# Sliding-window scores in four 64x64 array tiles, with a narrower key band and two shifted copies of V

## The chip, the cores and the metric

The kernel runs on one core of a Trainium2 chip. The metric is the device time of one execution in microseconds (us), lower is better. A run's state is fast or slow, judged by its time against the fastest of the same kernel; only fast runs are compared here.

## The reference

Attention with a window of 128 keys and an ALiBi bias (8 batches, 8 heads, 576 positions, 64 wide), followed by a feed-forward step on the 4608 tokens:

```python
rel    = pos[:, None] - pos[None, :]
bias   = slopes[:, None, None] * (-np.abs(rel))[None]
mask   = (rel >= 0) & (rel < 128)
scores = np.where(mask, q @ k.T / sqrt(64) + bias, -1e9)     # per batch and head
attn   = softmax(scores)
x      = (attn @ v), heads side by side                      # 4608 x 512
h      = x @ w_in                                            # 512 -> 2048
out    = (h * np.cos(h)) @ w_out                             # 2048 -> 512
```

## The kernel before

All operations are listed first; then a small scheduler inside the kernel (`Plan`) plays them through in its own clock and fixes, for good, the order of the instructions on each engine. For that it uses **booked durations** that stand with each operation: `occ` is the time until the engine can take the next one, `lat` the time until the result is there. At run time there is no other order: each engine runs its list from the front, and stops where an operand is not ready.

```python
def op(self, eng, fn, r=(), w=(), dma=None, occ=100, lat=None, pri=5, ...):   # list one operation
...
    o.start = st                     # in schedule(): the booked times, and with them the order
    free[e] = st + o.occ
    ...
        o.end = st + o.lat
```

A batch of attention has eight units of a head pair and 256 queries, four with G = 0 (the first 256 positions) and four with G = 1, and a tail of 64 queries. They go in groups of three through scores (TensorE), exp (ScalarE), mask (VectorE), PV (the product of the exponentials, P, with V; TensorE) and norm (VectorE). Between these steps TensorE runs **filler**: the large matmuls of the feed-forward step, in chunks of 512 tokens.

```python
def scores(us):                                          # two row tiles, x = 0, 1: the two heads of a pair
    ...
    jobs = [(128, 384, 2 * G, 2 * G, 2), (384, 512, 2 * G + 1, 2 * G + 1, 1)]
    if G:
        jobs.append((0, 128, 2 * G - 1, 2 * G, 1))
    for (c0, c1, kc, qb, nb) in jobs:
        for x in range(2):
            ins = e.matmul(ps[:, banks[x], c0:c1], keys_ap(i, x, pr, kc),
                           query_ap(i, x, pr, qb, nb), start=True, stop=True)
    ...
    occ += 250 if u[0] == "t" else 220 if u[1] else 165

def mask(b, u):                                          # G = 1: one instruction; G = 0: two
    ...
    op("dve", lambda e: e.tensor_tensor(p, p, m, ALU.mult), ..., occ=605, lat=lat, pri=1)

def pv(b, u, s):                                         # per query block: diagonal and previous key block
    ...
    ins = e.matmul(o, P[i][:, x, d0:d0 + 128], V[:, kc, h, 0:65], start=True, stop=not two)
    if two:
        ins = e.matmul(o, P[i][:, x, p0:p0 + 128], V[:, kc - 1, h, 0:65], start=False, stop=True)
```

V is loaded one to two batches ahead, by DMAs that GpSimd issues, behind certain transposes:

```python
if c == 1:
    load_v(2, after=crossed[3:4])
    load_qk(3)
    load_v(3)
...
if 3 < c + 2 < B:
    load_v(c + 2, after=xops[3:4] if c > 2 else xops[-1:])
```

The softmax here doesn't subtract the row's maximum and nothing guards it: scores larger than these inputs give would overflow.

## Time and profile before

Median of three runs 313.91 us (313.4 to 314.86). The profiled execution has a span of 311.4 us at a granted clock of 1.0.

| | before |
|---|---|
| TensorE busy | 302.1 us, 97% of the span |
| VectorE busy | 196.8 us, 63% |
| ScalarE busy | 206.7 us, 66% |
| share of the chain that ended last | TensorE 86%, DMA 8%, VectorE 1% |
| first scores of batches 2 to 7 start at | 73.16, 104.47, 134.78, 165.62, 198.73, 229.43 us |

"The chain that ended last" is followed back from the last instruction, at each step to whatever released it. A chain that is nearly all TensorE means that the other engines are in time nearly everywhere. Batches count from 0. (The prediction calls the batch at 134 us "batch 5"; it is batch 4. Nothing hangs on it. Where it speaks of a score group "before and after the change alike", it means the change of tiling mode at the group's two ends.)

### The profile page before, as it was taken

To read this page: it belongs to the slowest core of one execution; us is meant where nothing else is said; L and a number is where in the kernel's file an instruction comes from. 1 tells how busy PE (TensorE), PEld (TensorE's weight loads), DVE (VectorE), ACT (ScalarE), POOL (GpSimd) and SP (SyncE) were. 2 spreads that over 40 slices of the span, in tenths; PEclk is the share of its full clock that TensorE was granted. 3 is DMA by queue.
4 is the path that set the end of the run, shared out by engine and by line. 5 is a ranking of instruction groups with operands and counts; after the bars stand their busy time and mean duration, and the time that the engine had idled before them with its cause. 6 is when DMAs were issued, how large, how long until landed. Compare 5 with 4: busy or idle time off the path is not lost.

```text
span 311.4 us, 6714 instructions
## 1 busy us (share of the span) xinstructions
PE 302.1 (97%) x2647; PEld 178.0 (57%) x2684; DVE 196.8 (63%) x444; ACT 206.7 (66%) x303; POOL 105.8 (34%) x134
## 2 busy tenths in 40 slices
PE   8799999999999999999999999999999999999996
PEld 4578546785578557845854554455445544444444
DVE  3798675786568757875887458766866882353000
ACT  7798936787588759773986488848873884462211
POOL 8999820069506300870537055505000000000000
DMA  9999999999939992999999999999823200101112
GB/s 131 166 193 193 192 171 193 164 105 167 189 76 121 154 171 47 120 152 191 141 175 158 176 138 108 147 169 138 144 59 103 70 8 2 68 0 67 69 67 101
DMA packets 159742, 38.97 MB, mean 125 GB/s; under 512 B 147808, under 2 KB 155232, under 8 KB 159712
## 3 DMA queue, kind: packets, MB, share of 16 engines
q0 software_dynamic: 109552, 18.10, 80.0%
q1 hardware_dynamic: 50160, 20.46, 33.5%
q8 instruction: 21, 0.34, 0.5%
q14 instruction: 9, 0.07, 0.1%
HBM read 36.70 MB, written 9.44 MB: 148 GB/s over the span
## 4 chain that ended last, share of the span: by engine, by line
PE 86%; DMA 8%; POOL 3%; issue 1%; DVE 1%; ACT 0%; POOLq 0%
PE ps L863 37%; PE ps L837 20%; PE ps L852 18%; DMA qnat<-in_q_dram 6%; PE ps L631 4%; PE ps L725 3%; DMA knat<-in_k_dram 2%; PE ps L728 2%; POOL vp L463 1%; PE ps L800 1%; PE ps L711 1%; PE ps L546 1%; PE ps L713 1%; PE ps L621 1%; POOL qnat L427 0%
## 5 line engine op out<-in xcount | busy, mean ns | idle before, releaser
L863 PE MATMUL ps<-w_outb,gT 128*128 128x512 bf16 (+2 forms) x564 | 133.7, 373 | 2.2 <-issue 0.8
L829 DVE TENSOR_TENSOR gT<-ps,cos 128x512 bf16<-128x512 f32 x144 | 94.8, 686 | 27.7 <-PE ps L863 14.0
L823 ACT ACTIVATE cos<-ps,halfpi 128x512 f32<-128x512 f32 x144 | 94.9, 687 | 20.9 <-PE ps L837 6.7
L863 PEld LDWEIGHTS ps<-w_outb,gT 128*128 128x128 bf16 x592 | 52.6, 98 | 53.1 <-issue 1.4
L668 ACT ACTIVATE p<-ps 128x768 bf16<-128x768 f32 (+1 forms) x64 | 54.8, 919 | 27.5 <-PE ps L631 15.3
L852 PE MATMUL ps<-xT,w_inb 128*128 128x256 bf16 x576 | 67.5, 273 | 0.0
L837 PE MATMUL ps<-xT,w_inb 128*128 128x512 bf16 x280 | 63.9, 379 | 0.6
L463 POOL DMA_DIRECT2D vp<-in_v_dram x40 | 34.8, 909 | 79.8 <-DMA xT<-xnat 35.2
L852 PEld LDWEIGHTS ps<-xT,w_inb 128*128 128x128 bf16 x576 | 54.5, 98 | 7.2 <-issue 0.5
L837 PEld LDWEIGHTS ps<-xT,w_inb 128*128 128x128 bf16 x288 | 27.3, 98 | 32.2 <-DVE xtail L756 1.1
L419 ACT ACTIVATE ob<-ps 128x512 f32<-128x512 f32 (+2 forms) x24 | 14.0, 582 | 44.2 <-PE ps L863 44.2
L454 POOL DMA_DIRECT2D qnat<-in_q_dram x32 | 29.3, 915 | 26.1 <-DMA xT<-xtail 26.1
L686 DVE TENSOR_TENSOR p<-p,emask 128x1024 bf16<-128x1024 bf16 x32 | 22.0, 688 | 13.7 <-ACT p L668 13.5
L454 POOL DMA_DIRECT2D knat<-in_k_dram x32 | 29.3, 917 | 2.1 <-PE ps L713 2.1
L767 DVE TENSOR_TENSOR xnat<-ps,rec 128x256 bf16<-128x256 f32 x64 | 26.8, 421 | 2.0
L725 PEld LDWEIGHTS ps<-vp,p 128*128 128x128 bf16 x256 | 17.0, 97 | 15.0 <-issue 8.8
L725 PE MATMUL ps<-vp,p 128*128 128x65 bf16 x256 | 21.9, 193 | 0.5 <-DVE p L686 0.4
L691 DVE TENSOR_TENSOR p<-p,emask 128x256 bf16<-128x256 bf16 x32 | 9.1, 283 | 17.6 <-ACT p L668 17.1
L728 PE MATMUL ps<-vp,p 128*128 128x65 bf16 x192 | 20.0, 193 | 0.0
L491 ACT ACT_TABLE_LOAD x15 | 19.2, 1283 | 0.3
L631 PEld LDWEIGHTS ps<-qt,kt 64*128 64x128 bf16 x320 | 12.0, 95 | 11.5 <-issue 7.8
L631 PE MATMUL ps<-qt,kt 64*128 64x128 bf16 (+1 forms) x320 | 18.4, 241 | 0.1
(58 smaller groups left out, 173.8 us busy)
## 6 DMA issues: line engine op xcount, KB each, us to landing
out_dram<-ob SPq DMA_DIRECT2D x35, 256.0 KB, 3.8
vp<-in_v_dram POOLq DMA_DIRECT2D x32, 128.0 KB, 5.9
knat<-in_k_dram POOLq DMA_DIRECT2D x25, 128.0 KB, 8.9
qnat<-in_q_dram POOLq DMA_DIRECT2D x25, 128.0 KB, 7.7
w_inb<-in_moe_w_in_dram POOLq DMA_DIRECT2D x8, 256.0 KB, 9.0
w_outb<-in_moe_w_out_dram POOLq DMA_DIRECT2D x6, 256.0 KB, 15.1
qnat<-in_q_dram POOLq DMA_DIRECT2D x3, 256.0 KB, 10.6
knat<-in_k_dram POOLq DMA_DIRECT2D x3, 256.0 KB, 13.3
```

The costliest lines, as they stand in the source:

```text
L454: op("pool", [lambda e: e.dma_start(nat[w][b % 2][0:rows, t, :].rearrange("p (h d) -> p h d", h=H), src[b, :, 128 * t:128 * t + rows, :].r ...
L463: op("pool", [lambda e, t=t, rows=rows: e.dma_start(vp[b % 2][0:rows, t, :, 0:64], v[b, :, 128 * t:128 * t + rows, :].rearrange("h p d -> ...
L631: ins = e.matmul(ps[:, banks[x], c0:c1], keys_ap(i, x, pr, kc), query_ap(i, x, pr, qb, nb), start=True, stop=True)
L668: op("act", lambda e: e.activation(P[i][:, :, lo:512], src_[:, :, lo:512], ACTF.Exp, scale=0.125), w=held + [("P", i)], occ=920 if u[1] el ...
L725: ins = e.matmul(o, P[i][:, x, d0:d0 + 128], V[:, kc, h, 0:65], start=True, stop=not two)
L728: ins = e.matmul(o, P[i][:, x, p0:p0 + 128], V[:, kc - 1, h, 0:65], start=False, stop=True)
L767: op("dve", lambda e: e.tensor_tensor(o, U[:, :, :, 0:64], rv[:, :, :, None].broadcast_to([128, 2, 2, 64]), ALU.mult), r=[("rec", ri)], w= ...
L823: op("act", lambda e: e.activation(cosb[ci][:, :], h, ACTF.Sin, bias=halfpi[:, 0:1]), r=["halfpi"], w=[("B", bank), ("cos", ci)], occ=586, ...
L829: op("dve", lambda e: e.tensor_tensor(o, h, cs, ALU.mult), r=[("cos", ci)], w=[("B", bank)] + keys, occ=606, lat=692, pri=3)
L837: op("pe", lambda e, kc=kc: e.matmul(ps[:, bank, :], w_in[:, kc, 128 * fc:128 * fc + 128], xT[:, kc, CH * c:CH * c + CH], start=(kc == 0), ...
L852: op("pe", lambda e, i=i, fc=fc, kc=kc: e.matmul(ps[:, bank, 256 * i:256 * i + 256], w_in[:, kc, 128 * fc:128 * fc + 128], xT[:, kc, t0:t0 ...
L863: op("pe", lambda e, fc=fc: e.matmul(ps[:, bank, 0:wd], gT[gi][:, fc, 128 * t:128 * t + 128], w_out[:, fc, c0:c0 + wd], start=(fc == 0), s ...
```

## The change

Its intent: a block of 128 queries needs at most 255 keys, but a block of 64 queries needs only 191. Cut the queries in blocks of 64, and a band of 192 keys does. Scores, exp and masks then touch 192 in place of 256 keys per query, and the scores run in four 64x64 tiles of the array in place of two 64x128. The keys of a query block now start at multiples of 64, so PV needs V shifted by 64 positions too: `vx`, made by four VectorE copies per batch. The part of P that belongs to only one half of a block is masked into a zeroed tile `Ph`, by instructions on 64 partitions. Batches 0 and 1 stay as they were. The core of the diff, with cuts marked by "..." and three comments added:

```diff
+QUART = 2
+        Ph = [sb(f"ph{i}", [128, 2, 2, 128]) for i in range(NH)]
+        vx = sb("vx", [128, 6, H, VW])
+        def dense_masks(behind):                           # set-up, once, ahead of batch 2
+            for j in range(2):
+                ... e.tensor_copy(EM[a:a + 64, :, 256:384], EM[a:a + 64, :, c:c + 128]) ... occ=330, lat=400, pri=6
+            for i in range(NH):
+                ... e.memset(Ph[i][:, :, :, :], 0.0) ... occ=200, lat=270, pri=6
+        def shifted_v(b):                                  # V's shifted copies, four per batch
+            for j in range(2):
+                a = 64 * j
+                for n, (o, t) in enumerate(((0, 1 - j), (3, j))):
+                    op("dve", lambda e, a=a, o=o, t=t: e.tensor_copy(
+                        vx[a:a + 64, o:o + 3, :, :], V[a:a + 64, t:t + 3, :, :]),
+                       ... occ=480, lat=560, pri=4)
         def scores(us):
+                    if b >= QUART:
+                        for pr, j, c, kb, ks, qb, q0, n in quarters(b, u):
+                            for x in range(2):
+                                rows = slice(64 * x, 64 * x + 64)
+                                ins = e.matmul(ps[64 * j:64 * j + 64, banks[x], c:c + n],
+                                               tr["k"][i][rows, kb, pr, 64 * ks:64 * ks + 64],
+                                               tr["q"][i][rows, qb, pr, q0:q0 + n], ...)
         def mask(b, u):                                    # the G = 1 case
+                    e.tensor_tensor(p[:, :, :, 0:128], p[:, :, :, 0:128], EM[... 256:384] ..., ALU.mult)
+                    for j in range(2):
+                        a = slice(64 * j, 64 * j + 64)
+                        ins = e.tensor_tensor(
+                            Ph[n][a, :, :, 64 * j:64 * j + 64], p[a, :, :, 128:192],
+                            EM[a, hh, None, 192 * j:192 * j + 64].broadcast_to([64, 2, 2, 64]), ALU.mult)
+                op("dve", f, ..., occ=750 if G else 620, lat=835 if G else 705, pri=1)
         def pv(b, u, s):
+                            e.matmul(o, P[i][:, x, 192 * rb:192 * rb + 128],
+                                     vx[:, Q - 1, h, 0:65], start=True, stop=False)
+                            ins = e.matmul(o, Ph[hbuf[(b, u)]][:, x, rb, :],
+                                           vx[:, Q + 2, h, 0:65], start=False, stop=True)
+                    if c + 1 == QUART:
+                        dense_masks([o for o in R.all if o.eng[0] == "dve"][-1:])
...
+                    shifted_v(c + 1)
```

## The prediction

> **What bounds the kernel now.** I read the page's busy shares first, then the chain that ended last, then the groups by shape, and last the timelines of TensorE and VectorE around one batch (batch 5, from 134 us). From the page, the busy shares and the chain by engine:
>
> ```profile
> PE 302.1 (97%) x2647; PEld 178.0 (57%) x2684; DVE 196.8 (63%) x444; ACT 206.7 (66%) x303; POOL 105.8 (34%) x134
> ...
> PE 86%; DMA 8%; POOL 3%; issue 1%; DVE 1%; ACT 0%; POOLq 0%
> ```
>
> TensorE is the bound: 97% busy, and 86% of the chain. The other engines have a third of the span free. So TensorE time saved counts in full, while work added to VectorE is free only as long as no TensorE instruction has to wait for it. The groups that the change touches, from the groups by shape (count | busy us, mean ns of one | idle before):
>
> ```profile
> L668 ACT ACTIVATE p<-ps 128x1024 bf16<-128x1024 f32 x32 | 31.0, 1026 | 13.3 <-PE ps L621 11.9 <-PE ps L631 1.4
> L668 ACT ACTIVATE p<-ps 128x768 bf16<-128x768 f32 x32 | 24.4, 812 | 14.1 <-PE ps L631 13.9
> L686 DVE TENSOR_TENSOR p<-p,emask 128x1024 bf16<-128x1024 bf16 x32 | 22.0, 688 | 13.7 <-ACT p L668 13.5
> L631 PE MATMUL ps<-qt,kt 64*128 64x256 bf16 x128 | 15.4, 277 | 0.1
> L631 PE MATMUL ps<-qt,kt 64*128 64x128 bf16 x192 | 14.6, 218 | 0.0
> L693 DVE TENSOR_TENSOR p<-p,emask 128x512 bf16<-128x512 bf16 x32 | 13.4, 419 | 0.0
> L691 DVE TENSOR_TENSOR p<-p,emask 128x256 bf16<-128x256 bf16 x32 | 9.1, 283 | 17.6 <-ACT p L668 17.1
> ```
>
> The whole of the scores is only 30.0 us of overlapping matmul time in 311 us, so nothing here can be large. TensorE's timeline for the first score group of batch 5 (start, length, what) gives its real cost:
>
> ```profile
> 134.78 0.67 PE L631 MATMUL ps<-qt,kt 64*128 64x256 bf16 x12
> 135.38 1.90 PE L863 MATMUL ps<-w_outb,gT 128*128 128x512 bf16 x8
> 137.12 0.26 PE L725 MATMUL ps<-vp,p 128*128 128x65 bf16 x3
> ...
> 140.24 0.78 PE L631 MATMUL ps<-qt,kt 64*128 64x256 bf16 x16
> 140.95 0.82 PE L863 MATMUL ps<-w_outb,gT 128*128 128x512 bf16 x3
> ```
>
> Read start to start: the group of three G=0 units holds TensorE from 134.78 to 135.38, 0.60 us, the second group (one G=0, two G=1) 0.71 us. Filler (L863) runs while ScalarE and VectorE work, then the PV matmuls (L725) come. VectorE at the same place:
>
> ```profile
> 136.33 0.29 DVE L691 TENSOR_TENSOR p<-p,emask 128x256 bf16<-128x256 bf16 x1 [1.10 <-ACT p L668]
> 136.54 0.42 DVE L693 TENSOR_TENSOR p<-p,emask 128x512 bf16<-128x512 bf16 x1
> 137.03 0.29 DVE L691 TENSOR_TENSOR p<-p,emask 128x256 bf16<-128x256 bf16 x1
> 137.24 0.42 DVE L693 TENSOR_TENSOR p<-p,emask 128x512 bf16<-128x512 bf16 x1
> 137.57 0.18 DVE L765 RECIPROCAL rec<-ps 128x4 f32<-128x4 f32 x1
> ```
>
> The first mask ends at 136.54 + 0.42 = 136.96 and its PV starts at 137.12: 0.16 us later. Over all 72 units that distance is 0.06 to 0.25 us nearly everywhere. The static order puts each PV just where its mask is ready, and within a group VectorE works without a gap. **There is almost no slack between a mask and its PV**, though VectorE is only 63% busy.
>
> **What the Trainium skill says.** "TensorEngine Tiling (Array Packing)", Key Properties: tiles run independently, and a change of tiling mode drains the array. The trace agrees with the second: about 0.1 us is lost on each side of a score group, before and after the change alike. "TensorE: Matmul & The Clock Gate", Part 3, has row and column tiles compose; this trace shows two row tiles (scores) and two column tiles (the 32 transposes from 47.08 to 48.10 us start 0.03 us apart, half of what 128 columns take), never four tiles. "VectorE: DVE Perf Modes", the perf-mode tier table: 16-bit tensor_tensor gets two elements a cycle, a copy within SBUF four. The masks agree: 256, 512 and 1024 elements take 283, 419 and 688 ns, 0.53 ns per element and 0.15 us fixed. The same page, "Two Vector instructions with no wait between them": an instruction whose operands start in another 32-partition quadrant than those of the one before is held until all earlier ones have finished. Nearly all of this kernel starts at partition 0; the one case with a start at 64 is a memset at the beginning (third column "DVE", then line):
>
> ```profile
> 1.42 0.27 DVE L513 MEMSET vp<- 64x256 uint32 x1
> 1.77 0.09 DVE L515 MEMSET ptail<- 128x32 uint32 x1
> 1.83 0.17 DVE L516 MEMSET kt<- 128x128 uint32 x1
> ```
>
> The one after the partition-64 memset starts 0.08 us behind its end, the next starts 0.03 us before the end of its predecessor. That agrees, but another memset pair with no such change also waited, so the trace does not settle it.
>
> **The change part by part** (batches 2 to 7, so six times; each has four G=0 and four G=1 units and a tail).
>
> Scores, TensorE. Before, each of two row tiles streams 384 columns for a G=0 and 512 for a G=1 unit. After, each of four tiles streams 320 and 384. The tail stays at 512 (32 small matmuls for 16). Per batch 4 x 64 + 4 x 128 = 768 columns less. A column costs 0.42 ns (512-column matmuls start 0.216 us apart). So 0.32 us a batch, **1.9 us in all**, if four tiles really run side by side. The number of matmuls rises by 10 per G=1, 8 per G=0 and 16 per tail: 88 x 6 = 528, each with a weight load. They cost start time (about 3 ns between partners), so I count 1.5 us. PV keeps its count and its 65 columns: 0. Mode switches: as many as before.
>
> Exp, ScalarE: 1024 to 768 elements takes 1026 to 812 ns; 768 to 640, at the same 0.84 ns per element, 812 to 705. Per batch 4 x 0.214 + 4 x 0.107 = 1.28 us, 7.7 us in all, off the path.
>
> Masks, VectorE. G=1: one 688 ns instruction becomes three: 512 elements (419) and two of 256 on 64 partitions (283 each), 985 in sum. G=0: 283 + 419 = 702 becomes 419 + 2 x 221 (128 elements: 0.15 us + 128 x 0.53 ns) = 861. Per batch 4 x 0.30 + 4 x 0.16 = 1.8 us. V's copies: 4 a batch of 1584 elements, at four a cycle 412 ns + 0.15 = 0.56 us, 2.2 us a batch. In all 24 us more, plus 2 us of set-up: VectorE from 197 to about 223 us, 71%. Not the bound as a total.
>
> But each mask lies between exp and PV. In the old kernel instructions overlap: a 256-element mask's successor starts 0.21 us after it (136.33 to 136.54), 0.07 less than its length. The scheduler that fixes the order books 0.62 us (G=0) and 0.75 us (G=1) per new mask, which is what the three would take with such overlaps. Two of the three start at other partitions than their predecessor (64 after 0, and 0 after 64). If these are held, each loses the overlap of some 0.09 us: a mask ends 0.09 us later than booked, and the next VectorE instruction starts 0.18 us later. In a group of three masks in a row the third is late by 2 x 0.18 + 0.09 = 0.45 us. With a further 0.07 us after an end, as in the memsets, it is 0.7. TensorE executes in order, so it stands still for that, less up to 0.08 us of slack: 0.35 to 0.65 us a group. Three groups in six batches: **6 to 12 us of new waits**. If nothing is held: about 0 to 1 us.
>
> Sum: held, -1.5 + 6 to 12 = +4.5 to +10.5. Not held, -1.5 + 0.5 = -1.
>
> **The rivals.**
> 1. The scores get shorter, nothing waits: 312 to 313 us. For it: TensorE is the bound, ample filler. Against: the tight distance from mask to PV above.
> 2. The masks arrive late and TensorE stands still before PV: 318 to 324 us. For it: the static order without slack and the held rule. Against: the rule is barely visible in this trace; filler matmuls may be ordered with more room than I think. I give this about 65%, with a part only of the reckoned wait being the likeliest.
> 3. Four tiles don't run side by side, or 16 short matmuls and 16 loads per unit are bound by issue: at 20 ns a matmul a G=1 unit takes 0.32 in place of 0.22 us, a G=0 unit 0.24 in place of 0.165: +4 us. Against: two column tiles start 3 ns apart here. 10%.
> 4. V's copies come late in batch 2: its V loads are issued from 65.05 to 69.3 us and land about 6 us later, the masks start at 74.7; the copies stand ahead of them on VectorE. About 1 us, once.
>
> **Range and chances.** Rival 1 (a third) is centred on 312.7, rival 2 (most of the rest) on about 319. Their mixture has its middle near 317, so I predict 317 us, 1% slower, with 8 in 10 between 312 and 323. Faster by over 2% (below 307.6) would need three times what the scores can give: 0.01. Slower by over 2% (above 320.2) needs the upper half of rival 2, or 2 and 3 together: 0.27. The rest, 0.72, within 2%.
>
> **What would show it.** Right on scores: the groups take about 0.5, 0.6 and 0.67 us from start to the next matmul. Right on the masks: within a mask the second partition-64 instruction starts at or after the end of the first, the next instruction again after its end, and PV groups show TensorE gaps above 0.216 us behind filler whose end is a mask, growing from first to third unit. Wrong: those gaps are as before and the span is 1 to 2 us shorter (rival 1), or score groups are longer than before (rival 3). VectorE should show about 223 us, ScalarE about 199.

## The result, and the profile after

The changed kernel takes **331.65 us** (median of four runs, 330.96 to 332.07), 18.0 us more. The ratio is 1.0565, with a 95% interval of 1.0528 to 1.0602. (Ratios here are the mean time of one kernel's fast runs over that of the other's of the same rounds, so not quite the ratio of the medians.) The predicted range ended at 323.

The page of the changed kernel: busy shares, the granted clock in 40 slices (the page of the kernel before has no such row, since its trace records no lowered clock), and the chain by engine.

```profile
PE 309.4 (94%) x3172; PEld 178.1 (54%) x3212; DVE 220.7 (67%) x541; ACT 202.8 (61%) x308; POOL 106.1 (32%) x134
...
PEclk9699999997799999998999999999999999999999
...
PE 65%; DVE 15%; DMA 8%; ACT 4%; POOL 3%; issue 3%; SPq 0%; DVEq 0%; POOLq 0%; ACTq 0%
```

VectorE (DVE) is as busy as predicted, two thirds of the span, so it is no bound as a total. But its share of the chain went from 1% to 15%: TensorE now waits for single VectorE results. The clock row has dips that the kernel before did not have. The groups by shape that answer to those of before (count | busy us, mean ns of one | idle before, and what ended it):

```profile
L554 DVE COPY vx<-vp 64x1584 bf16<-64x1584 bf16 x24 | 15.8, 660 | 4.6 <-DMA vp<-in_v_dram 4.3
...
L765 DVE TENSOR_TENSOR ph<-p,emask 64x256 bf16<-64x256 bf16 x48 | 13.6, 283 | 0.3
...
L664 PE MATMUL ps<-qt,kt 64*64 64x128 bf16 x384 | 10.6, 222 | 3.1 <-DVE gT L938 2.5 <-DVE xnat L876 0.4
...
L814 PE MATMUL ps<-vp,p 128*128 128x65 bf16 x48 | 5.7, 201 | 5.2 <-DVE ph L756 4.9
```

Read the last column: PV of the G = 0 units (L814) has 5.2 us of idle time before it, 4.9 of it ended by a mask (`ph`; 4.2 of this is one single wait, the second place below), and the scores (L664) 3.1 us, most of it ended by `gT`, a product of the feed-forward step on VectorE. V's copies (L554) take 660 ns each; they were booked 480, and predicted 560. Three places in the timelines show what happened.

**1. The masks.** VectorE in batch 2 (start, length in us, what): a G = 1 mask (L760, then two L765 on 64 partitions) and the next instruction.

```profile
89.69 0.43 DVE L760 TENSOR_TENSOR p<-p,emask 128x512 bf16<-128x512 bf16 x1
90.04 0.58 DVE L765 TENSOR_TENSOR ph<-p,emask 64x256 bf16<-64x256 bf16 x2
90.65 0.18 DVE L874 RECIPROCAL rec<-ps 128x4 f32<-128x4 f32 x1
```

The first of the 64-partition instructions, which starts at partition 0 like its predecessor, overlaps it (90.04 is before 89.69 + 0.43). But two of 283 ns take 0.58 us: the second, at partition 64, starts 14 ns after the end of the first. The next one, back at partition 0, starts 31 ns after the end of that. So the mask keeps VectorE for 0.95 us (from 89.69 to 90.65) where the scheduler booked 0.75; a G = 0 mask takes 0.82 where it booked 0.62. TensorE meets this as waits like the following, in front of the third PV of a group (183.60 us, batch 5), where the filler that the static order put there ended too early:

```profile
182.75 0.60 PE L972 MATMUL ps<-w_outb,gT 128*128 128x512 bf16 x2
183.60 0.22 PE L814 MATMUL ps<-vp,p 128*128 128x65 bf16 x2 [0.26 <-DVE ph L756]
```

I summed such waits over the trace: the time from where the columns of the matmul before end (0.42 ns a column) to the first matmul of a PV, from 70 us on, where it is between 0.04 and 0.8 us. The kernel before has 11 of them, 1.2 us; the changed one 51, **9.95 us**. Three of the 51, 0.64 us together, lie in stretches of half clock (see below): there the matmul before was slower, and no mask was late. Within a group the waits grow from unit to unit, as the prediction said they would: 0.05, 0.21 and 0.42 us in the group that the fence is taken from.

**2. Batch 2 starts late.** VectorE:

```profile
74.17 3.65 DVE L554 COPY vx<-vp 64x1584 bf16<-64x1584 bf16 x4 [1.16 <-DMA vp<-in_v_dram]
77.83 1.59 DVE L541 COPY emask<-emask 64x1024 bf16<-64x1024 bf16 x2
79.52 0.55 DVE L546 MEMSET ph<- 128x256 uint32 x2
80.10 0.43 DVE L752 TENSOR_TENSOR p<-p,emask 128x512 bf16<-128x512 bf16 x1
```

TensorE, the changed kernel at the same place:

```profile
75.62 1.24 PE L972 MATMUL ps<-w_outb,gT 128*128 128x512 bf16 x5
81.03 0.27 PE L814 MATMUL ps<-vp,p 128*128 128x65 bf16 x2 [4.17 <-DVE ph L756]
```

and the kernel before:

```profile
73.76 1.90 PE L863 MATMUL ps<-w_outb,gT 128*128 128x512 bf16 x8
75.50 0.26 PE L725 MATMUL ps<-vp,p 128*128 128x65 bf16 x3
```

In the kernel before, the first PV of batch 2 came at 75.50 and needed only the first two blocks of V; the copies need four. In the changed kernel VectorE stops at 73 us for a V that has not landed, then makes four copies (3.65 us; booked 4 x 0.48 = 1.92), then the mask set-up (2.1 us), and only then the first mask. TensorE has no work listed ahead of that PV any more and stands still for 4.2 us.

**3. Batch 4 starts late.** VectorE, then TensorE:

```profile
145.26 0.72 DVE L554 COPY vx<-vp 64x1584 bf16<-64x1584 bf16 x1 [2.14 <-DMA vp<-in_v_dram]
145.91 0.67 DVE L938 TENSOR_TENSOR gT<-ps,cos 128x512 bf16<-128x512 f32 x1
```

```profile
146.72 0.62 PE L664 MATMUL ps<-qt,kt 64*64 64x128 bf16 x36 [2.31 <-DVE gT L938]
```

Here the copy stands in front of a product of the feed-forward step (`gT`, L938) that has nothing to do with V. The copy waits 2.14 us for V, the product waits behind it, and the scores wait for the product, whose bank of PSUM (the memory that matmuls write to) they take. One late operand on an in-order engine holds up everything listed behind it.

The two long waits have a sequel: the trace grants TensorE half its clock for 6.8 us from 79.1 us and for 3.4 us from 147.4 us (512-column matmuls then start 0.43 us apart, not 0.22). The Trainium skill ("TensorE: Matmul & The Clock Gate", Part 1, What's actually happening) says that the clock falls to half after an idle window of about 3.4 us, with windows that run free. The trace agrees with the length: its stretches of either clock last 3.41 us or multiples of it. It does not agree with a window that is idle throughout. When the clock fell at 79.15 us, TensorE had stood still for 2.3 us, not yet for 4.2; the wait in batch 4 was 2.3 us in all. In both cases about 2.3 of the 3.41 us before the fall were idle.

Where the time went, by the start of each batch's first scores:

| interval, from first scores of a batch to those of the next | before | after | more |
|---|---|---|---|
| start to batch 2 | 73.16 | 73.33 | 0.2 |
| batch 2 | 31.31 | 39.58 | 8.3 |
| batch 3 | 30.31 | 33.81 | 3.5 |
| batch 4 | 30.84 | 32.69 | 1.9 |
| batch 5 | 33.11 | 35.09 | 2.0 |
| batch 6 | 30.70 | 31.60 | 0.9 |
| batch 7 to the end | 81.97 | 84.10 | 2.1 |

(The wait before the first scores of batch 4 falls into the row of batch 3.)

A reckoning of the 18.8 us between the two profiled spans: 0.2 at the start; mask waits 9.95 - 0.64 - 1.2 = 8.1; the two long waits 4.3 + 2.5 = 6.8 (by the same reckoning as the mask waits); scores -1.2 (below). That is 13.9. The half clock adds at most about 4 us, an estimate (10.2 us at half clock, less 1.9 us of them in which TensorE still stood still, halved). The sum does not prove this part. The four runs had granted clocks of 0.974, 0.979, 0.990 and 0.990, so by an estimate some 17, 14, 7 and 7 us at half clock, and took 332.07, 332.01, 330.96 and 331.29 us: ten microseconds less of half clock made only about 1 us. So 1 to 4 us stay without a shown place.

### The profile page after: what moved, and what is told of

It is laid out like the page before. It is cut to its first block, busy times and chain, and to the rows that moved or that the text cites. A ratio compares the mean times of both kernels' runs of the same rounds, so it can differ in the third digit from the quotient of the medians.

```text
span 330.2 us, 7862 instructions
## 1 busy us (share of the span) xinstructions
PE 309.4 (94%) x3172; PEld 178.1 (54%) x3212; DVE 220.7 (67%) x541; ACT 202.8 (61%) x308; POOL 106.1 (32%) x134
## 4 chain that ended last, share of the span: by engine, by line
PE 65%; DVE 15%; DMA 8%; ACT 4%; POOL 3%; issue 3%; SPq 0%; DVEq 0%; POOLq 0%; ACTq 0%
PE ps L972 29%; PE ps L946 16%; PE ps L961 10%; DMA vp<-in_v_dram 6%; PE ps L664 4%; ACT p L723 3%; DVE ph L765 2%; DVE p L760 2%; DVE vx L554 2%; POOL vp L467 2%; DVE gT L938 2%; DMA kt<-knat 1%; DVE p L752 1%; DVE ph L756 1%; DVE ptail L737 1%
## 5 line engine op out<-in xcount | busy, mean ns | idle before, releaser
L972 PE MATMUL ps<-w_outb,gT 128*128 128x512 bf16 (+2 forms) x561 | 136.3, 380 | 3.3 <-issue 2.4
L938 DVE TENSOR_TENSOR gT<-ps,cos 128x512 bf16<-128x512 f32 x144 | 94.3, 686 | 25.0 <-PE ps L972 15.2
L423 ACT ACTIVATE ob<-ps 128x512 f32<-128x512 f32 (+2 forms) x30 | 17.5, 584 | 52.6 <-PE ps L972 52.6
L723 ACT ACTIVATE p<-ps 128x640 bf16<-128x640 f32 (+1 forms) x48 | 33.1, 757 | 25.0 <-PE ps L664 24.8
L458 POOL DMA_DIRECT2D qnat<-in_q_dram x32 | 28.5, 891 | 34.8 <-DMA xT<-xtail 33.9
L752 DVE TENSOR_TENSOR p<-p,emask 128x512 bf16<-128x512 bf16 x24 | 10.2, 424 | 15.3 <-ACT p L723 14.9
L760 DVE TENSOR_TENSOR p<-p,emask 128x512 bf16<-128x512 bf16 x24 | 10.2, 426 | 14.1 <-ACT p L723 13.6
L554 DVE COPY vx<-vp 64x1584 bf16<-64x1584 bf16 x24 | 15.8, 660 | 4.6 <-DMA vp<-in_v_dram 4.3
L729 ACT ACTIVATE p<-ps 128x768 bf16<-128x768 f32 (+1 forms) x16 | 14.0, 918 | 6.2 <-PE ps L684 6.2
L664 PEld LDWEIGHTS ps<-qt,kt 64*64 64x64 bf16 x864 | 10.6, 108 | 11.1 <-issue 11.0
L817 PE MATMUL ps<-vx,p 128*128 128x65 bf16 x144 | 15.5, 196 | 1.0
L817 PEld LDWEIGHTS ps<-vx,p 128*128 128x128 bf16 x144 | 10.6, 99 | 10.3 <-DVE ph L765 4.2
```

The source lines that it names most:

```text
L458: op("pool", [lambda e: e.dma_start(nat[w][b % 2][0:rows, t, :].rearrange("p (h d) -> p h d", h=H), src[b, :, 128 * t:128 * t + rows, :].r ...
L554: op("dve", lambda e, a=a, o=o, t=t: e.tensor_copy(vx[a:a + 64, o:o + 3, :, :], V[a:a + 64, t:t + 3, :, :]), r=[("v", i, t + k) for k in r ...
L664: ins = e.matmul(ps[64 * j:64 * j + 64, banks[x], c:c + n], tr["k"][i][rows, kb, pr, 64 * ks:64 * ks + 64], tr["q"][i][rows, qb, pr, q0:q0 ...
L723: op("act", lambda e: e.activation(P[i][:, :, lo:384], src_[:, :, lo:384], ACTF.Exp, scale=0.125), w=held + [("P", i)], occ=700 if u[1] el ...
L817: e.matmul(o, P[i][:, x, 192 * rb:192 * rb + 128], vx[:, Q - 1, h, 0:65], start=True, stop=False)
L938: op("dve", lambda e: e.tensor_tensor(o, h, cs, ALU.mult), r=[("cos", ci)], w=[("B", bank)] + keys, occ=606, lat=692, pri=3)
```

## The experiments

Two theories stood at first. **A**: the masks cost the time, because the held 64-partition instructions are longer than booked. **B**: the copies cost it, because V lands too late for them. The rival to both, "theory C" in the expectations, is that VectorE simply has too much work. In what follows, "mask waits" are the sum defined above, "long waits" those over 0.8 us before a PV or scores. One caution holds for all of it: a changed booking or load makes the scheduler plan the whole order anew, so filler moves between batches in every run, and how much a new plan by itself moves the time was not tested.

| label | what it is | median us | ratio to before | mask waits, us |
|---|---|---|---|---|
| | before | 313.65 | 1 | 1.2 |
| | after | 331.65 | 1.0565 | 9.95 |
| e1_flat_masks | after, no 64-partition masks | 321.45 | 1.0247 | 1.2 |
| e2_rebooked_masks | after, masks booked as measured | 322.24 | 1.0265 | 3.55 |
| e3_early_v | after, V loaded earlier | 325.85 | 1.0392 | 9.9 |
| e5_flat_and_early | e1 and e3 | 317.87 | 1.0154 | 2.35 |
| e6_flat_early_no_copies | e5, copies for batch 2 only | 316.98 | 1.0124 | 2.3 |
| e8_best_mix | e5, fewer masks, copies booked 0.57 | 318.0 | 1.0142 | 1.9 |
| e10_rebooked_all | after, all VectorE additions booked as measured | 321.7 | 1.0285 | 3.2 |
| e11_rebooked_all_early_v | e10 and e3 | 315.77 | 1.0097 | 3.7 |
| e12_from_batch_3 | change from batch 3 on, several mends | 316.54 | 1.0111 | 1.55 |
| e14_all_mended | e2, V partly earlier, set-up earlier, copies booked 0.60 | 318.56 | 1.0182 | 3.1 |
| e15_all_mended_070 | e11, set-up earlier | 315.27 | 1.0082 | 2.95 |
| e16_overbooked | e15, masks and copies booked with room | 313.11 | 1.0006 | 0.13 |
| e4_old_plus_copies | before, and the copies | 318.99 | 1.0181 | 1.3 |
| e7_old_copies_early_v | e4, V loaded earlier | 318.76 | 1.0198 | 0.85 |
| e9_old_early_v | before, V loaded earlier | 312.82 | 0.999 | |
| e13_old_copies_booked | e7, copies booked 0.70 | 314.73 | 1.0064 | 1.8 |

The runs of the kernel before beside the experiments had medians of 312.9 to 313.2 us. For e9 the waits are not given, since its profiled run was slow.

### e1: masks without a change of partitions

The two small mask instructions run on all 128 partitions with a zero-padded mask, kept in an unused part of P. They write zeros where `Ph` has to be zero. Bookings unchanged.

```diff
-                            Ph[n][a, :, :, 64 * j:64 * j + 64], p[a, :, :, 128:192],
-                            EM[a, hh, None, 192 * j:192 * j + 64].broadcast_to([64, 2, 2, 64]),
-                            ALU.mult)
+                            Ph[n][:, :, :, 64 * j:64 * j + 64], p[:, :, :, 128:192],
+                            P[pr][:, :, None, 384 + 64 * j:448 + 64 * j].broadcast_to(
+                                [128, 2, 2, 64]), ALU.mult)
```

> The changed kernel, but the two small instructions of each mask run on all 128 partitions (against a mask with zeros) in place of 64 each: as many instructions and elements per partition, but every start is at partition 0, so nothing is held; bookings unchanged. Theory A (held masks cost TensorE 0.3 to 0.4 us a group): a mask takes 0.62 and 0.75 us to the next instruction in place of 0.82 and 0.95, the gaps of 0.28 to 0.43 us before PV vanish, and the chunks of batches 3, 5, 6 and 7 get 1.5 to 2 us shorter each: about 322 us. The waits for V in batches 2 and 4 stay. Theory C (VectorE simply has too much work per batch): no change in those chunks, 331 us.

321.45 us (320.18 to 321.8): 10.2 us less than the changed kernel. VectorE's timeline shows a G = 1 mask:

```profile
94.66 0.42 DVE L765 TENSOR_TENSOR p<-p,emask 128x512 bf16<-128x512 bf16 x1
95.00 0.49 DVE L769 TENSOR_TENSOR ph<-p 128x256 bf16<-128x256 bf16 x2
95.40 0.18 DVE L879 RECIPROCAL rec<-ps 128x4 f32<-128x4 f32 x1
```

The same number of instructions on twice the partitions takes 0.49 in place of 0.58 us for the pair, and the mask 0.74 in place of 0.95 us: nothing is held any more, and the booking of 0.75 is right. The mask waits are back at 1.2 us. Theory A holds. Number and width along the free axis are the same; the start partitions differ, and the number of partitions. That the latter is not what holds is seen in the changed kernel: of its two 64-partition instructions the one at partition 0 starts 83 ns ahead of the end before it, and only the one at 64 waits.

### e2: the masks as they are, booked as they are

```diff
-                   w=[("P", i), ("Ph", n)], occ=750 if G else 620, lat=835 if G else 705, pri=1)
+                   w=[("P", i), ("Ph", n)], occ=950 if G else 820, lat=922 if G else 788, pri=1)
```

> The changed kernel with the same instructions; only the scheduler's bookings of a mask are set to what the trace shows (0.82 and 0.95 us to the next instruction in place of 0.62 and 0.75), so that it orders more filler before PV. Theory A in its form 'order without slack, filler is ample': the gaps before PV vanish just as in the run with flat masks, about 323 us, though each mask takes as long as before. Theory C (work, not order): 331 us.

322.24 us (319.82 to 322.77): 9.4 us less, though each mask is as long as before (0.95 and 0.82 us in its trace). So what the masks cost is neither VectorE's throughput nor the hold in itself. The static order was made with wrong numbers; with right ones the scheduler lists more filler ahead of each PV, and most of the hold is hidden (3.55 us of mask waits are left). The rival "too much VectorE work" falls for the masks here; for the whole change, only with e16.

Both e1 and e2 gain more than the mask waits they remove (8.7 and 6.4 us). They also have a shorter wait in batch 2 (2.6 and 3.3 in place of 4.3 us), though a new one of 1.4 and 1.0 us before a PV of batch 4, and less half clock in mid-kernel (3.4 and 0 us in place of 10.2). The two causes seem to share that part.

### e3: V loaded earlier

```diff
-                        load_v(2, after=crossed[3:4])
-                        load_qk(3)
+                        load_v(2)
+                        load_qk(3, crossed[3:4])
...
-                    load_v(c + 2, after=xops[3:4] if c > 2 else xops[-1:])
+                    load_v(c + 2, after=xops[3:4])
```

> The changed kernel with V of batches 2 and 4 loaded earlier (batch 2 without waiting for the third key transpose, batch 4 behind the fourth output transpose in place of the last one; the q and k loads stay where they were). Theory B (copies wait for V at the head of VectorE's queue, everything behind them and then TensorE waits, and TensorE then runs at half clock): the idle 4.2 and 2.3 us and both half-clock stretches vanish, the chunks of batches 2 and 4 fall by 4 to 5 us each, about 322 us. Rival: the DMA queues are full and V lands as late, or transposes get late in its place: 327 us or more. The gaps of 0.28 to 0.43 us before PV stay in both.

325.85 us (325.13 to 326.18): 5.8 us less, about half of what I expected. The half-clock stretches in mid-kernel are gone, and of the long waits two of 0.9 us remain, both around batch 2. The mask waits are untouched (9.9 us). So late V costs about 6 us in the changed kernel, and not the 9 to 10 that the missed expectation (322 us) held.

### e4 and e9: the copies alone, and the early V alone, in the kernel before

e4 adds the 24 copies to the kernel before, where nobody reads them; e9 is the kernel before with only the edit of e3.

```diff
+        vx = sb("vx", [128, 6, H, VW])
+        def shifted_v(b): ...           # as in the change
+                    shifted_v(c + 1)
```

> The kernel before with the 24 V copies added at the same places and nothing that reads them: no small array tiles, no narrow band, old masks. Theory B: the copies alone, waiting for V in batch 2 and perhaps batch 4, stop VectorE and then TensorE: 318 to 322 us. Theory A alone (masks are all of it): within 1 us of the kernel before, 314 us.

318.99 us (318.47 to 320.06), 5.8 us more than the kernel before, with waits of 1.4 us before the first PV of batch 2 and of 1.6 and 0.9 us in batch 4. The copies are far from free even where nothing needs their result.

> Control: the kernel before with only V of batches 2 and 4 loaded early, no copies. The unused copies cost the kernel before 5.8 us with late V and 5.9 with early V, against my theory that the wait for V is their cost. If early V by itself is free: 313 us, then the copying itself costs 5.9. If early V itself costs some us (transposes and loads get late): 315 to 318, then the copying costs less than it seems.

312.82 us in its three fast runs (ratio 0.999, interval 0.9965 to 1.0016): loading V earlier costs nothing in the kernel before.

### e5 and e6: both mends, and both without copies

> The changed kernel with flat masks and early V together. Flat masks alone took 10.2 us off the changed kernel, early V alone 5.8. If the two costs are separate they add: 331.65 - 16 = 315.7 us, still some 2.5 us over the kernel before. If they share a part (a VectorE that is late for one reason is late anyway): 318 us or more.

317.87 us (316.87 to 319.17). Against e3 the flat masks are worth 8.0 us here, where neither trace has a half-clock stretch in mid-kernel: the cleanest figure for theory A. Together they gain 13.8, not 10.2 + 5.8 = 16.0; the 2.2 us would be the shared part of above. Left are 1.9 us before the first scores of batch 2, ended by a `gT` product, and 1.7 us before filler at 131 us, ended by the DMA that brings transposed tokens.

e6 drops the copies for batches 3 to 7, so its result is wrong:

```diff
-                    shifted_v(c + 1)
+                    if c == 1:
+                        shifted_v(c + 1)
```

> As the run before, but V's copies are made for batch 2 only and batches 3 to 7 reuse them: a wrong result on purpose. It shows what the small array tiles and the narrow band are worth when VectorE neither holds nor copies. Theory: what is left over the kernel before is the copies' own work; without it the score groups' 0.2 us a batch show: 312 us, 1 us under the kernel before. Rival: some other cost of the small tiles (weight loads, issue) is left: 314 us or more.

316.98 us (316.05 to 317.44), a miss: I expected 312. The 20 copies that were dropped are worth 0.9 us here, which the ranges of the two runs do not separate; a wait of 2.4 us ahead of the first scores of batch 2 stays, where the other four are. In the profiles, the first scores of batch 3 start 3.8 us later than in the kernel before, and the end comes 3.2 us later. So in this form what is left stands at batch 2.

### e7 and e13: why copies cost time with V loaded early

e7 is e4 with V loaded early. If waiting for V were all that the copies cost, this kernel would be as fast as the one before.

> The kernel before with the 24 unused V copies, and V of batches 2 and 4 loaded early. With late V these copies cost 5.8 us. If the wait for V is what costs, not the copying: 313.5 to 314.5 us. If the copying itself (16 us of VectorE in busy stretches) costs: 317 us or more.

318.76 us (317.68 to 321.77), a miss: the cost stays at 6 us. The wait moved. TensorE around the first scores of batch 2, then VectorE:

```profile
71.66 0.59 PE L874 MATMUL ps<-w_outb,gT 128*128 128x512 bf16 x2
74.38 0.86 PE L642 MATMUL ps<-qt,kt 64*128 64x256 bf16 x12 [2.13 <-DVE gT L840]
```

```profile
70.95 0.57 DVE L540 COPY vx<-vp 64x1584 bf16<-64x1584 bf16 x1
71.54 1.29 DVE L840 TENSOR_TENSOR gT<-ps,cos 128x512 bf16<-128x512 f32 x2
72.84 0.69 DVE L540 COPY vx<-vp 64x1584 bf16<-64x1584 bf16 x1
73.54 0.69 DVE L840 TENSOR_TENSOR gT<-ps,cos 128x512 bf16<-128x512 f32 x1
```

The scores wait for the last `gT` products. VectorE is busy without a pause at that place: copies that were booked 0.48 us and took 0.57 and 0.69 us stand between those products, and everything behind them comes later than the order assumed. Late V is not quite gone, though: VectorE stands still for it for 1.6 us before its first copy at 66.9 us and for 1.3 us at 162.5 us. So this run alone does not separate the wait from the copying. e13 changes only the booking:

```diff
-                       w=[("vx", n, j)], occ=480, lat=560, pri=4)
+                       w=[("vx", n, j)], occ=700, lat=780, pri=4)
```

> The kernel before with early V and the unused copies, which cost 5.9 us so far, now booked at 0.70 us each in place of 0.48. Early V alone is free (312.8 us). In the run with 0.48 booked, scores stood 4.6 us in four places behind the last product of a chunk, which the copies had delayed. Order theory: those waits vanish with the right booking, 313 to 314.5 us. Work theory (copies do not fit beside the products): 317 us or more again.

314.73 us (314.23 to 316.04), just over the range of the order theory: 4.0 of the 5.9 us are gone, with the same copies. VectorE stands still for V no less than in e7 (1.7 and 2.1 us, at two copies), and before the first scores of batch 2 a wait of 1.3 us in place of 2.3 is left. So it is the booking again: the order with more room loses less to such stops and to long copies.

### e8, e10 and e11: bookings of everything, with and without early V

e8 joins flat masks (with one instruction fewer for G = 0), early V and copies booked 0.57.

> The changed kernel with early V, flat masks, the two small instructions of a G=0 mask merged into one (0.56 us booked), and the copies booked at the 0.57 us that they take. Theory: every known wait is gone: 313 to 315 us, so at best even with the kernel before, since the scores can give only about 1.2 us.

318.0 us (315.52 to 318.38), a miss: waits of 1.6 and 1.2 us at the start of batch 2 remain. The copies are not the reason: those of batch 2 took 0.55 to 0.57 us, as booked. But VectorE stood still for V for 1.1 us before the first of them (66.3 us), and the set-up of the masks ahead of the first mask took 3.6 us, where its instructions were booked 2.2 us.

e10 is the changed kernel with every VectorE addition booked as the trace shows it (masks 0.95 and 0.82, copies and mask copies 0.70, memsets 0.27), e11 the same with early V.

> The changed kernel, same instructions, with masks (0.95 and 0.82 us), V copies (0.70 in place of 0.48), mask set-up (0.70 in place of 0.33) and clearing (0.27 in place of 0.20) all booked as long as the traces show them. If all that is lost is the order's wrong idea of VectorE, the copies' part goes too: 317 us or less (masks alone rebooked gave 322.2). If the wait for late V or the work itself is what is left: 320 us or more.

> As the run before with early V as well. Order theory: 314 to 316 us, the waits behind the last VectorE product of a chunk (1.8 to 2.3 us before the first scores of batch 2 with early V) fall below 1 us. Work theory (the copies do not fit beside the products in the stretch where they are put): 317 to 318 us, like flat masks with early V (317.9).

321.7 us (321.01 to 323.19) and 315.77 us (315.69 to 316.69). Right bookings alone leave the late V, with 2.8 us before the scores of batch 4, and gain next to nothing over e2, where the masks alone were rebooked (322.24 us). Early V is then worth 5.9 us. With both, no long wait is left by this count, and the kernel is 1% slower than the one before. (One of 1.1 us before filler, for transposed tokens, is left at 131.6 us.)

### e12 and e14: two that missed

e12 begins the change at batch 3, with flat masks, copies booked 0.60, and V of batch 4 loaded after an earlier transpose than in the changed kernel, but not as early as in e3. e14 is e11 with the mask set-up moved ahead of batch 1, copies booked 0.60, and V of batch 4 a little later than in e3.

> Small tiles and narrow band from batch 3 only, so that set-up and first copies do not fall into the stretch around 70 to 79 us; flat masks, one instruction for the small part of a G=0 mask, copies booked at 0.60, V of batch 4 behind the sixth output transpose. Five batches save 0.2 us of scores each. If batch 2's copies and set-up are the rest of the loss: 312 to 313.5 us, even with the kernel before or 0.3% under it. If each batch's copies cost: 315 us or more.

> The changed kernel with early V for batch 2, V of batch 4 behind the seventh output transpose, masks booked as they run, copies booked at 0.60 us, and the mask set-up moved to where VectorE has time (before batch 1). The run with all booked and early V stood 0.8 us before batch 2's first PV (set-up) and 1.1 us behind an output transpose of batch 3; both should go: 313.5 to 314.5 us. Faster than the kernel before only if no other wait takes their place: 312.

316.54 us (314.95 to 317.8) and 318.56 us (318.21 to 319.76). The traces show late V in both. In e12 VectorE stands still for V of batch 3, whose load was not moved, for 2.9 us before the first copy (88.03 us), and a PV of batch 2 waits 1.5 us behind it; before the first copy for batch 4 (134.75 us) it stands 3.5 us, and TensorE then waits 2.0 us before filler and 0.8 us before the first scores of batch 4, for `gT`. In e14 it stands 2.5 us for V of batch 4 (135.25 us), and the first scores of batch 4 wait 2.4 us, again for a `gT` product; those of batch 2 wait 1.5 us, behind a stop of 1.4 us for V and a copy of 0.84 us that was booked 0.60. In both several things differ at once, so no run separated each cause by itself.

### e15 and e16: bookings with room

e15 is e14 with copies booked 0.70 and V as early as in e3. e16 differs from e15 only in that the numbers are larger than measured:

```diff
-                       w=[("vx", n, j)], occ=700, lat=780, pri=4)
+                       w=[("vx", n, j)], occ=900, lat=980, pri=4)
-                   w=[("P", i), ("Ph", n)], occ=950 if G else 820, lat=922 if G else 788, pri=1)
+                   w=[("P", i), ("Ph", n)], occ=1030 if G else 900, lat=1000 if G else 870, pri=1)
```

> As the run with everything mended, but copies booked at 0.70 us (not 0.60) and V of batch 4 early (behind the fourth output transpose, not the seventh). That run stood 1.5 and 2.4 us before the first scores of batches 2 and 4, behind the last product of the chunk. If the short booking and the later V caused that: 314 to 315.5 us, 0.3 to 1 us under the run with all booked and the set-up left where it was (315.8). If it is the moved set-up: 317 us or more.

> The same with every mask booked 0.08 us and every copy 0.20 us longer than it takes, so that the order has room where the old one had none. Order theory: what is left of short waits (0.19 us at some PVs) goes as well, 313.5 to 315 us. Work theory (VectorE has 20 us more to do, and the rest of 2 to 3 us is where it is the slowest engine for a while): no gain, 315 us or more.

315.27 us (315.07 to 316.24) and **313.11 us** (312.3 to 313.84; ratio 1.0006, interval 0.9987 to 1.0024). e16 does all that the changed kernel does: the same 864 score matmuls in 64x64 tiles, the same 144 mask instructions with their holds, and 24 copies. It also has V early and the set-up moved. It is even with the kernel before, 18.5 us faster than the changed one. Its busy shares, then TensorE at the start of batch 2:

```profile
PE 299.0 (96%) x3172; PEld 178.2 (57%) x3212; DVE 217.4 (70%) x540; ACT 201.1 (65%) x309; POOL 106.5 (34%) x134
```

```profile
72.70 2.12 PE L972 MATMUL ps<-w_outb,gT 128*128 128x512 bf16 x8
74.66 0.23 PE L814 MATMUL ps<-vp,p 128*128 128x65 bf16 x2
...
74.84 0.81 PE L972 MATMUL ps<-w_outb,gT 128*128 128x512 bf16 x3
75.49 0.23 PE L814 MATMUL ps<-vp,p 128*128 128x65 bf16 x2
```

Between two PVs of a group there are now three filler matmuls where the changed kernel had two (the fence at 182.75 us), and PV starts as they end. VectorE still stands still for V for 1.2 us before its first copy (66.2 us), and nothing waits for that. VectorE's 20 us more work is hidden: 0.13 us of mask waits are left. What is gained in the scores (1.2 us) and in mask waits (1.1 us against before) is used up elsewhere; among others, its trace has 1.1 us before feed-forward matmuls that wait for transposed tokens, which I did not follow further. No version of the changed kernel was faster than the kernel before. No run booked the old masks of the kernel before with more room, so whether that kernel, with its 1.2 us of mask waits, would gain too is open.

### The copies beside GpSimd

The 16 profiled kernels with copies hold 360 of them. The 169 during which GpSimd issued no load took 514 to 572 ns, 558 on average. The 191 that overlapped such an issue took 552 to 1086 ns, 661 on average, and 74 of them more than 620. In batch 2 of the changed kernel all four did, with 1021, 862, 865 and 861 ns. The Trainium skill has a mechanism for it ("SBUF — State Buffer", Who interferes with whom): VectorE in the fast two-port copy mode and GpSimd share a port pair as an exclusive lock, and who comes second waits for the whole instruction of the other. The two groups agree with it. Many overlapping copies lost nothing, which the page would put down to their being first. A longer copy is also likelier to overlap an issue. No experiment took the issues away, so this remains an association here.

## Why the prediction was wrong

- **Scores, -1.5 us: right.** From the start of a group to the next matmul, the three groups of a batch take 0.55, 0.62 and 0.73 us; before, 0.60, 0.71 and 0.78. (In the last two a matmul behind the group has a weight load in the trace but no record, and its 0.23 us are taken out; that much lies between first groups with this record, 0.55 us, and without, 0.78.) That is 0.20 us a batch, 1.2 us in all. Four tiles do run side by side, and rival 3 is out.
- **ScalarE and VectorE totals: right in size, in part by luck.** ScalarE 202.8 us (predicted about 199), VectorE 220.7 (about 223). The exps saved 7.8 us, as reckoned (7.7), but six more evacuations of outputs ran on ScalarE (30 for 24, 3.6 us more) and six fewer on VectorE (7 for 13, 4.2 us less). Without that VectorE's additions come to about 28 us, not the 26 predicted; the copies alone took 15.8 in place of 13.4.
- **Held masks, 6 to 12 us: right where the text computed it, and then not believed.** The hold is as described, with 14 and 31 ns behind an end. It gave about 8 us of waits (8.1), and 8.0 us of time where no half clock interfered (e3 to e5). (A slip in the working: with a further 0.07 us at each hold the third mask of a group is late by 0.8 us, not 0.7.) The text gave this rival 65% "with a part only of the reckoned wait being the likeliest", which put the middle at 317. The masks and scores alone would have made about 313.7 + 8.1 - 1.2 = 321 us, an estimate, which lies in the predicted range.
- **The step that failed is rival 4: "the copies stand ahead of them on VectorE. About 1 us, once."** Measured, late V cost 5.8 us (e3), at two places: TensorE stood still for 4.2 us in batch 2 and 2.3 us in batch 4, and half clock came with each. Several things went wrong in it. It did not enter the sum at all. Even by its own figures 1 us is little: a last load issued at 69.3 us and landing 6 us later, then four copies of 0.56 us, bring the first mask to as late as 77.5 us, 2.8 us after the 74.7 named. It priced the copies' work and V's landing, but not what stands behind them in the static order: the mask set-up that VectorE does next (2.1 us), and in batch 4 a product that TensorE's scores need. It took "once" from batch 2 without looking at when V lands for batch 4. And it took 0.56 us per copy from an undisturbed rate, where these four took 0.86 to 1.02.
- **What was missing altogether: the booked numbers as a cause of their own.** The text saw that the mask's booking assumes an overlap, but did not apply the same question to the copies (booked 0.48, taking 0.66) or to the mask copies of the set-up (booked 0.33, taking 0.79). In the kernel before, the copies' booking alone is worth 4.0 us (e7 to e13).
- The outcome was not VectorE as a bound. e16 shows that: the same work, listed by numbers with room and with V early, costs nothing against the kernel before.

What stays open: where the last 1 to 4 us of the 18.8 lie, how the last 2.2 us from e15 to e16 divide between masks and copies, why e5, e8, e11 and e15, all with V of batch 4 early, wait 1.1 to 1.7 us for transposed tokens at about 130 us, how much of each gain is a new plan's luck, and whether fewer loads issued by GpSimd would make the copies short.

## What to carry to other kernels

Where a static order is made from assumed durations and the engines run it in order, a change that adds instructions to an engine with a third of its time free can still cost several per cent, because each instruction that is longer than booked, or whose operand is late, holds up what stands behind it. Measure each new kind of instruction in place, beside its real neighbours, and book it with some room: bookings longer than measured by 0.08 us (masks) and 0.3 us (copies, which took 0.59 us on average in e16) cost nothing here, masks booked 0.2 us too short cost 8 us. Ask of every new operand when it lands in each batch, and what unrelated work is listed behind the one that waits for it.

## What the Trainium skill lacked or had wrong

- "VectorE: DVE Perf Modes", Two Vector instructions with no wait between them: the rule of the hold was right, but the page has no size for it. Here a held instruction started 14 ns (64x256 and 64x128, partition 64 behind 0) or 31 ns (partition 0 behind 64) after the end of the one before, where an instruction that is not held starts about 83 ns ahead of that end.
- "TensorE: Matmul & The Clock Gate", Part 1, What's actually happening: it has the clock fall after at least one idle window of about 3.4 us. Here no window was idle throughout: in the changed kernel both falls in mid-kernel came after 3.41 us of which about 2.3 were idle. In e1, e7, e10 and e14 falls in mid-kernel came after windows with 2.1, 2.1, 1.8 and 2.3 us idle, while one with 2.0 us in e2 had no fall.
- "TensorEngine Tiling (Array Packing)": four 64x64 tiles do run side by side; the drain at a change of mode has no figure there, and here it is about 0.1 us on each side of a score group.
- "SBUF — State Buffer": it has the lock between VectorE's copies and GpSimd, but no figure for a bf16 copy beside the issue of loads; here 64x1584 copies took 552 to 1086 ns in place of 514 to 572.
